# Dummy matmuls around the slots' matmuls: 38 on a constant cleared once, in place of 11 on one cleared there

## The chip, the cores and the metric

The kernel runs on one core of a Trainium2 chip. The metric is the device time of one execution in microseconds (us), lower is better. The engines are TensorE (PE in the rows; PEld is its weight load), VectorE (DVE), ScalarE (ACT), GpSimd (POOL) and SyncE (SP), which here issues most transfers. [...]

## What is computed

Three layers follow each other: attention with a sliding window and a few sink keys, a mixture of eight experts in which each token goes to one expert, and a feed-forward layer of two matrix products.

```python
# attention: batch 2, heads 8, sequence 768, head size 64, window 128, 4 sink keys
scores = where(is_sink | in_window, q @ k.T / sqrt(D), -1e9)
x = (softmax(scores) @ v).transpose(0, 2, 1, 3).reshape(1536, 512)
# experts: 8 of them, 512 -> 1024 -> 512
expert_idx = argmax(normed(x) @ normed(expert_emb).T / tau, axis=1)
for e in range(8):
    m = expert_idx == e
    out[m] = gate_w[m, None] * (maximum(x[m] @ w1[e], 0) @ w2[e])
# feed-forward: 512 -> 2048 -> 512, weights given as float64
h = out @ w_in
y = maximum(0.01 * h, h) @ w_out
```

## The kernel before

The program has three stages. The first, to about 147 us, is attention, with the router's logits, ranks and counts worked in at its end (`router_logits`, `router_rank`, `rank_experts`). It writes the tokens' rows to a buffer in DRAM, `xd`. The second runs the eight experts one after the other, each with a fixed capacity of tokens. The third is the feed-forward layer, in four chunks of 384 tokens.

Between the first and the second stage stands the list of slots: `route` works out which token stands in which slot of which expert, and `id_list` makes the list `ids` by twelve small matmuls (L791) over `c.u` (one-hot rows of the tokens) and `ata` (which block a token falls in, L785). VectorE copies the result to `ids` (L792). Behind that copy VectorE copies the expert's number once more, to `eid2` (L824), and from it SyncE computes the addresses of the first expert's weights from the second quarter on; the first quarter's two loads use `eid` and start earlier. GpSimd uses `ids` to gather the expert's rows from `xd`, 128 at a time, by indirect transfers (L1095).

Weights come in slots of 512 KB (L997), fourteen of which are in use at this point. For most experts each number is cut into a coarse and a fine part: ScalarE casts (L1001), VectorE subtracts (L1002). A product is then three matmuls (`pair`, L1079). The first expert has 128 tokens and runs in `moe_narrow`, in four chunks i. Chunk i's `up` is twelve matmuls into `hp` with slot 2i; ScalarE takes their maximum with zero to `hr` (L1222); `turn` transposes `hr` on TensorE into `th`, and ScalarE (L1230) and VectorE (L1231) cut it into the two parts of `h`; `down` is six matmuls into `acc` with slot 2i+1. `Flow` puts them in the order up 0, turn 0, up 1, down 0, turn 1, up 2, and so on. Ahead of that `turn_rows` transposes the gathered rows on TensorE (`tr`, L1068), and ScalarE and VectorE cut them into `mxT` (L1072, L1073). The rows of the next expert are gathered and turned between the chunks.

The order of the work has two sources. From the second stage on TensorE's instructions run in the order in which the program writes them (`manual_schedule`, L1486). Those of ScalarE, VectorE, GpSimd and SyncE are put in order at build by a planner (`schedule_with_timeline_sim`, L1526): it follows its own timeline and gives an engine, among the instructions that are ready there, the one that the program wrote first. The cuts of the first fourteen slots are written ahead of the first `turn_rows` (`c.work.pop(Q0)`, L1326). On the chip each engine then runs its queue strictly in that order.

`stir` (L1268) is a run of dummy matmuls, 128x128 weights by 512 columns, on a bf16 tile of zeros, whose result nobody reads. Its PSUM tile is one of the four `acc` buffers; their banks were the router's and the attention's until then. There are two places: `WARM[0]` of them ahead of the list's matmuls (L788), `WARM[1]` behind them and ahead of the first `tr` (L1328). The zeros are `c.hot`, cleared by GpSimd as the second stage opens (L1491), in memory of the first stage that has been given back. An attention `stir` of its own (L329) runs seven such matmuls at the very start, on `c.warm`, which VectorE clears at about 1 us (L233) and which lies in a pool of the attention.

Of the kernel before, what the change touches and what calls it, by code (L numbers as in the profile page):

```python
# [9 lines left out]
BF16 = mybir.dt.bfloat16  # L10
# [11 lines left out]
P = 128  # L22
# [116 lines left out]
def attention(c, ctx):  # L139
# [4 lines left out]
    att = ctx.enter_context(tc.tile_pool(name="a_qk", bufs=4))  # L144
# [9 lines left out]
    def load_qk(b, pr, c0=0, n=QB):  # L154
        rk, rq = raws[b, pr] = c.raws[pr % 2]
        for j in range(2):
            nc.sync.dma_start(out=rk[:, c0:c0 + n, j, :],
                              in_=c.k[b, 2 * pr + j].rearrange("(c p) d -> p c d", p=P)[:, c0:c0 + n])
        for j in range(2):
            for twice in range(2):  # L160
                nc.sync.dma_start(out=rq[:, c0:c0 + n, j, twice, :],
                                  in_=c.q[b, 2 * pr + j].rearrange("(c p) d -> p c d", p=P)[:, c0:c0 + n])
# [66 lines left out]
    switches(c, ctx)  # L229
    load_qk(0, 0, 0, 3)  # L230
    load_qk(0, 1, 0, 3)
    c.warm = att.tile([P, 512], BF16, tag="warm", name="warm", bufs=1)
    nc.vector.memset(c.warm, 0.0)  # L233
    setup(c)
    W3 = 2 * P + SINK
# [106 lines left out]
    first, second = group_turns(0, 0)  # L342
    setting = router_setup(c, ctx)
    stir(7)
    n = len(items)
    for _ in range(2):
        first.pop(0)()
    s = 0
    while s < n or after:
# [5 lines left out]
        if s < n:  # L355
            b, g, i, h = items[s]
            k = groups.index((b, g))
            if s in STIR:
                stir(STIR[s])
            j = TURN[b].index(i)  # L360
            at = 4 * j + h
            if s < 3:
                for _ in range(2):
                    if first:
                        first.pop(0)()
            if at in SECOND:
                second.pop(0)()
            if k + 1 < len(groups):
                nb, ng = groups[k + 1]
                if at == 5:  # L370
                    load_qk(nb, 2 * ng, 0, 3)
                    load_qk(nb, 2 * ng + 1, 0, 3)
                    first, then = group_turns(nb, ng)
                if at == 13:
                    load_qk(nb, 2 * ng, 3, 3)
                    load_qk(nb, 2 * ng + 1, 3, 3)
                    load_v(nb, ng)
                if at in FIRST:
                    first.pop(0)()
                if at == 23:  # L380
                    assert not first and not second
                    second = then
            score(b, g, i, h)
# [396 lines left out]
def id_list(c, T, u, q, c0, n, nm):  # L780
# [6 lines left out]
    if nm == "a":  # L787
        stir(c, WARM[0])  # L788
    ip = c.ptr.tile([P, n], F32, tag="tr", name="ip" + nm)
# [152 lines left out]
def slots(c):  # L942

    at = (c.nc.sbuf_usable_end - NSL * 8192) // 32 * 32
    c.slots = [Slot(c, k, at + k * 8192) for k in range(NSL)]
    c.big = c.nc.alloc_sbuf_tensor_at("slot_big", [P, 4096], F32R, offset=at + (NSL - 2) * 8192)[:]
    c.bigf = c.nc.alloc_sbuf_tensor_at("slot_bigf", [P, 4096], F32, offset=at + (NSL - 2) * 8192)[:]
    c.u = c.nc.alloc_sbuf_tensor_at("slot_u", [P, NTT, P], F16, offset=at + (NSL - 2) * 8192)[:]
    end, c.heads = at + (NSL - 2) * 8192, []
    for k in range(8):  # L950
        o = end - (k + 1) * 4 * (KW + 2 * S)
        c.heads.append((c.nc.alloc_sbuf_tensor_at(f"head_k{k}", [P, KW], F32R, offset=o)[:],
                        c.nc.alloc_sbuf_tensor_at(f"head_q{k}", [P, 2, S], F32R, offset=o + 4 * KW)[:]))
    o = end - 8 * 4 * (KW + 2 * S) - 6 * QB * D * 8
    c.raws = [(c.nc.alloc_sbuf_tensor_at(f"raw_k{k}", [P, QB, 2, D], F32, offset=o + 3 * k * QB * D * 8)[:],
               c.nc.alloc_sbuf_tensor_at(f"raw_q{k}", [P, QB, 2, 2, D], F32, offset=o + (3 * k + 1) * QB * D * 8)[:])
              for k in range(2)]
    c.loads, c.work = Loads(c.slots[:NSL - 2]), Work(c.tc)
# [123 lines left out]
def moe_x(c, q0, n, tag, whole=False):  # L1082

    if tag is None:
        xT = c.conv[0].tile([P, 2, 4, n], F32R, tag="dt", name=f"mxT{c.uid()}")
    elif tag == "xb":
        t = 1 if whole else 2
        xT = (c.bigf if whole else c.big)[:, 0:4 * t * n].rearrange("p (t k n) -> p t k n", t=t, k=4)
    else:
        xT = c.mo.tile([P, 1 if whole else 2, 4, n], F32 if whole else F32R, tag=tag, name=f"mxT{c.uid()}", bufs=1)  # L1090
    todo = []
    for k in range(-(-n // P)):
        w = min(P, n - k * P)
        t = c.mo.tile([P, DM], F32, tag="rows" if k < 3 else "y", name=f"rows{c.uid()}", bufs=3)
        c.nc.gpsimd.indirect_dma_start(out=t[0:w], out_offset=None, in_=c.xd[:, :],  # L1095
                                       in_offset=bass.IndirectOffsetOnAxis(ap=c.ids[0:w, q0 + k:q0 + k + 1], axis=0))
        todo.append(lambda t=t, k=k, w=w: turn_rows(c, xT, t, k * P, w, whole))
    return xT, todo
# [163 lines left out]
TAIL = 6  # L1262


WARM = [3, 8]


def stir(c, n):  # L1268

    if n:  # L1270
        t = c.pacc.tile([P, 512], F32, tag="acc", name=f"stir{c.uid()}")
        for _ in range(n):
            c.nc.tensor.matmul(t, lhsT=c.hot[:, 0:P], rhs=c.hot, start=True, stop=True)


def moe(c):
# [44 lines left out]
    def tag(n):  # L1321
        return "xb" if n % 2 else "xa"
# [4 lines left out]
    xT, todo = moe_x(c, BASE[0], WIDTH[0], tag(0), ORDER[0] in WHOLE)  # L1327
    stir(c, WARM[1])  # L1328
    for fn in todo:
# [132 lines left out]
def program(tc, q, k, v, n_sink, window, emb, tau, w1, w2, w_in, w_out, out):  # L1462
    c = Ctx()
    c.tc, c.nc = tc, tc.nc
    c.q, c.k, c.v, c.n_sink, c.window = q, k, v, n_sink, window
    c.emb, c.tau, c.w1, c.w2, c.w_in, c.w_out, c.out = emb, tau, w1, w2, w_in, w_out, out
    c.x, c.xT, c.ids_n = {}, {}, 0

    def uid():
        c.ids_n += 1  # L1470
        return c.ids_n

    c.uid = uid
    with ExitStack() as ctx:
        c.const = ctx.enter_context(tc.tile_pool(name="const", bufs=1))
        c.dram = ctx.enter_context(tc.tile_pool(name="dram", bufs=1, space=DRAM))
        c.xd = c.dram.tile([NT, DM], F32, name="xd")
        with ExitStack() as actx:
            c.masks = actx.enter_context(tc.tile_pool(name="masks", bufs=1))
            c.rt = actx.enter_context(tc.tile_pool(name="r_tile", bufs=2))  # L1480
            slots(c)
            with ExitStack() as bctx:
                if MAN:
                    bctx.enter_context(tc.manual_schedule(engines=MAN))
                attention(c, bctx)
        with tc.manual_schedule(engines={PE}), ExitStack() as mctx:  # L1486
            c.mo = mctx.enter_context(tc.tile_pool(name="m_wk", bufs=1))
            c.conv = [mctx.enter_context(tc.tile_pool(name=f"conv{i}", bufs=1)) for i in range(CONV)]
            c.yT = c.mo.tile([P, 4, YW], F32, name="yT")
            c.hot = c.mo.tile([P, 512], BF16, tag="y", name="hot", bufs=3)  # L1490
            c.nc.gpsimd.memset(c.hot, 0.0)  # L1491
            for kk in range(4):
                c.nc.scalar.activation(out=c.yT[:, kk], in_=c.rowi.to_broadcast([P, YW]), func=AF.Copy, scale=0.0)
            c.pacc = mctx.enter_context(tc.tile_pool(name="ps_acc", bufs=4, space=PSUM))
            c.ph = mctx.enter_context(tc.tile_pool(name="ps_h", bufs=2, space=PSUM))
            c.ptr = mctx.enter_context(tc.tile_pool(name="ps_tr", bufs=2, space=PSUM))
            with ExitStack() as rctx:
                route(c, rctx)
                moe(c)
            c.conv.append(mctx.enter_context(tc.tile_pool(name="convx", bufs=1)))  # L1500
            ffn(c)
        rare = c.nc.values_load(c.rare[0:1, 0:1], min_val=0, max_val=1)
        with tc.If(rare > 0):
            general(c)
# [25 lines left out]
```

## Time and profile before

| what | us |
|---|---|
| three timed runs | 618.84, 621.79, 622.26 |
| their median | 621.79 |
| the profiled execution | 618.77 |
| span of the profiled execution, first to last instruction | 617.0 |
| TensorE busy with matmuls in that span | 588.9 |
| VectorE, ScalarE, GpSimd busy | 396.6, 292.9, 55.1 |

All rows below come from the one profiled execution. Times in them are counted from the first instruction. [...]

### The profile page before, as it was taken

What the parts mean: (1) busy time and instruction counts of PE and PEld (TensorE: products, weight loads), DVE (VectorE), ACT (ScalarE), POOL (GpSimd) and SP (SyncE); (2) the same over time, 40 slices, a digit from 0 to 9 for tenths busy, and PEclk for the clock granted to TensorE, in tenths of its full rate; (3) what the DMA queues carried; (4) which work ended last, traced back from release to release, by engine and by line L of the source; (5) the groups of instructions that cost most, each with busy time, mean ns of one, the idle gap of its engine ahead of it and who ended that gap; (6) DMA issues with size and microseconds to landing.
All of it is one profiled execution on the core that took longest, in us unless ns stands there. A gap on an engine that the chain in (4) does not pass through costs nothing.

```text
span 617.0 us, 10038 instructions
## 1 busy us (share of the span) xinstructions
PE 588.9 (95%) x3603; PEld 537.8 (87%) x3604; DVE 396.6 (64%) x953; ACT 292.9 (47%) x556; POOL 55.1 (9%) x156
## 2 busy tenths in 40 slices
PE   7899999997699999999999999799999999999996
PEld 4799999895599998889989998698998998899894
DVE  7889788856699659997973799953224322242230
ACT  4777787755687444524652463442223322332230
POOL 3011013003122010001000000010000100020001
PEclk7899999996699999999999999999999999999999
DMA  5777560013998683379499600000000100010001
GB/s 119 172 162 173 144 167 2 2 68 110 346 359 302 196 315 106 119 248 372 157 343 338 240 0 2 0 35 18 1 1 0 52 2 0 1 52 0 1 1 56
DMA packets 87994, 73.71 MB, mean 119 GB/s; under 512 B 54024, under 2 KB 70408, under 8 KB 87936
## 3 DMA queue, kind: packets, MB, share of 16 engines
q1 hardware_dynamic: 85824, 66.22, 34.4%
q0 software_dynamic: 2112, 6.75, 3.1%
q8 instruction: 31, 0.51, 0.4%
q14 instruction: 27, 0.22, 0.1%
HBM read 66.67 MB, written 6.29 MB: 118 GB/s over the span
## 4 chain that ended last, share of the span: by engine, by line
PE 87%; DVE 6%; DMA 2%; issue 2%; ACT 1%; SPq 1%; POOL 0%; POOLq 0%; DVEq 0%
PE acc L1079 30%; PE hp L1079 30%; PE xp L298 6%; PE sc L261 4%; PE hp L1176 3%; PE acc L1188 3%; PE tp L280 3%; DMA slot_raw<-in_moe_w 2%; PE tq L196 1%; PE lg L716 1%; PE xp L301 1%; PE tr L1068 1%; PE xTp L697 1%; PE tk L196 1%; DVE slot L1054 1%
## 5 line engine op out<-in xcount | busy, mean ns | idle before, releaser
L1079 PE MATMUL acc<-slot,h 128*128 128x512 f32 x603 | 151.8, 395 | 4.5 <-DVE slot L1054 3.4
L1079 PE MATMUL hp<-fxT,slot 128*128 128x384 f32 x768 | 142.3, 337 | 0.0
L1079 PEld LDWEIGHTS hp<-fxT,slot 128*128 128x128 f32 x768 | 134.9, 188 | 4.7
L1079 PEld LDWEIGHTS acc<-slot,h 128*128 128x128 f32 x603 | 111.8, 188 | 26.5 <-DVE slot L1054 4.1
L1424 DVE TENSOR_TENSOR lk<-hp,lk 128x384 f32<-128x384 f32 x64 | 35.5, 555 | 101.2 <-ACT lk L1423 101.2
L1423 ACT ACTIVATE lk<-hp 128x384 f32<-128x384 f32 x64 | 31.4, 491 | 126.2 <-PE hp L1079 119.3
L1002 DVE TENSOR_TENSOR slot<-slot_raw,slot 128x1024 fp32r<-128x1024 f32 x48 | 58.3, 1222 | 11.4 <-ACT slot L1001 11.1
L1001 ACT CAST slot<-slot_raw 128x1024 fp32r<-128x1024 f32 x48 | 50.0, 1047 | 18.1 <-DMA slot_raw<-in_moe_w 17.8
L268 ACT ACTIVATE p<-p,los 128x288 f32<-128x288 f32 (+2 forms) x96 | 45.6, 504 | 16.8 <-DVE los L266 16.2
L1079 PE MATMUL acc<-h,slot 128*128 128x256 f32 (+2 forms) x288 | 49.0, 319 | 0.0
L1426 DVE TENSOR_TENSOR h<-lk,h 128x384 fp32r<-128x384 f32 x59 | 32.7, 555 | 24.4 <-ACT h L1425 24.4
L261 PE MATMUL sc<-head_k,head_q 128*128 128x288 f32 (+1 forms) x192 | 43.9, 338 | 3.5 <-DVE head_k L207 1.1
L1079 PEld LDWEIGHTS acc<-h,slot 128*128 128x128 f32 x288 | 43.1, 188 | 2.9
L1425 ACT CAST h<-lk 128x384 fp32r<-128x384 f32 x59 | 30.2, 512 | 31.8 <-DVE lk L1424 31.8
L298 PE MATMUL xp<-v,pt 128*128 128x65 f32 x352 | 43.8, 269 | 0.0
L298 PEld LDWEIGHTS xp<-v,pt 128*128 128x128 f32 x352 | 42.6, 192 | 0.1
L1458 POOL DMA_INDIRECT out_y<-y,sid x12 | 12.4, 1037 | 318.6 <-DVE y L1457 298.4
L261 PEld LDWEIGHTS sc<-head_k,head_q 128*128 128x128 f32 x192 | 29.9, 201 | 6.9 <-ACT head_q L216 3.1
L1079 PE MATMUL hp<-slot_big,slot 128*128 128x256 f32 (+1 forms) x192 | 35.4, 333 | 0.0
L1079 PEld LDWEIGHTS hp<-slot_big,slot 128*128 128x128 f32 x192 | 29.8, 189 | 2.7
L280 PE MATMUL tp<-ident,p 128*128 128x128 f32 x176 | 30.2, 278 | 0.0
L1095 POOL DMA_INDIRECT rows<-xd,ids x16 | 18.6, 1162 | 114.0 <-PE tr L1068 110.7
(252 smaller groups left out, 842.6 us busy)
## 6 DMA issues: line engine op xcount, KB each, us to landing
slot_raw<-in_moe_w SPq DMA_DIRECT2D x56, 512.0 KB
slot_wide<-in_moe_w_in SPq DMA_DIRECT2D x8, 1024.0 KB
slot_wide<-in_moe_w_out SPq DMA_DIRECT2D x8, 1024.0 KB
raw_q<-in_q SPq DMA_DIRECT2D x64, 96.0 KB
slot_first<-in_moe_w SPq DMA_DIRECT2D x8, 512.0 KB
raw_k<-in_k SPq DMA_DIRECT2D x32, 96.0 KB
xd<-x SPq DMA_DIRECT2D x12, 256.0 KB
v<-in_v SPq DMA_DIRECT2D x12, 192.0 KB
```

What stands on the lines that cost most here:

```text
L261: nc.tensor.matmul(sc[:, 0:w], lhsT=qt[:, half, i * P:(i + 1) * P], rhs=kt[:, off:off + w], start=half == 0, stop=half == 1)
L268: later(1, lambda: nc.scalar.activation(out=p, in_=p, func=AF.Exp, scale=-1.0, bias=lo))
L280: nc.tensor.transpose(u.t[:, h % 2, n, :], u.p[:, h, o:o + P], c.ident)
L298: nc.tensor.matmul(xp[:, h, :], lhsT=u.pt[h // 2][:, h % 2, n, :], rhs=vT[b, g][:, kb, h, :], start=h == 0 and n == 0, stop=h == 3 and i < ...
L1001: nc.scalar.copy(out=sl.g[0], in_=sl.raw)
L1002: nc.vector.tensor_tensor(out=sl.g[1], in0=sl.raw, in1=sl.g[0].bitcast(F32), op=ALU.subtract)
L1079: c.nc.tensor.matmul(out, lhsT=a[x], rhs=b[y], start=first and n == 0, stop=last and n == 2)
L1095: c.nc.gpsimd.indirect_dma_start(out=t[0:w], out_offset=None, in_=c.xd[:, :], in_offset=bass.IndirectOffsetOnAxis(ap=c.ids[0:w, q0 + k:q0 ...
L1423: nc.scalar.activation(out=raw, in_=hp, func=AF.Copy, scale=0.01)
L1424: nc.vector.tensor_tensor(out=raw, in0=hp, in1=raw, op=ALU.max)
L1425: x = nc.scalar.copy(out=h[:, 0, :], in_=raw)
L1426: y = nc.vector.tensor_tensor(out=h[:, 1, :], in0=raw, in1=h[:, 0, :].bitcast(F32), op=ALU.subtract)
```

## The change

The constant on which the stirs of the second stage run is no longer `c.hot` but `c.warm`. `c.warm` moves from the attention's pool to the pool of constants, so that it lives to the end; `c.hot` and GpSimd's clear of it go. The stirs ahead of the list's matmuls become 10 where they were 3, and those behind them 28 where they were 8.

```diff
@@ -229,7 +229,7 @@
     load_qk(0, 1, 0, 3)
-    c.warm = att.tile([P, 512], BF16, tag="warm", name="warm", bufs=1)
+    c.warm = c.const.tile([P, 512], BF16, name="warm")
     nc.vector.memset(c.warm, 0.0)
@@ -1262,7 +1262,7 @@
-WARM = [3, 8]
+WARM = [10, 28]
@@ -1270,7 +1270,7 @@
         for _ in range(n):
-            c.nc.tensor.matmul(t, lhsT=c.hot[:, 0:P], rhs=c.hot, start=True, stop=True)
+            c.nc.tensor.matmul(t, lhsT=c.warm[:, 0:P], rhs=c.warm, start=True, stop=True)
@@ -1487,8 +1487,6 @@
             c.yT = c.mo.tile([P, 4, YW], F32, name="yT")
-            c.hot = c.mo.tile([P, 512], BF16, tag="y", name="hot", bufs=3)
-            c.nc.gpsimd.memset(c.hot, 0.0)
```

## Rows read from the trace of the kernel before

**Rows 1.** The page: its head, part 2's granted clock, part 4's chain by engine.

```profile
span 617.0 us, 10038 instructions
...
PEclk7899999996699999999999999999999999999999
...
PE 87%; DVE 6%; DMA 2%; issue 2%; ACT 1%; SPq 1%; POOL 0%; POOLq 0%; DVEq 0%
```

**Rows 2.** Chain that ended last, 147 to 164 us: start, duration, what.

```profile
148.85 0.70 POOL hot L1491
...
149.60 0.61 PE stir L1273
...
153.94 9.58 DMA slot_raw<-in_moe_w
```

**Rows 3.** Timeline, 146 to 155: start, duration, engine, line, operation [idle before <-releaser].

```profile
146.50 0.17 PE L733 MATMUL rk<-cum,ones 128*128 128x16 bf16 x1
...
146.80 0.16 DVE L736 TENSOR_TENSOR sel<-rk,oh 128x16 f32<-128x16 f32 x1
...
150.25 0.36 DVE L785 TENSOR_TENSOR ata<-qsel,q 128x192 f16<-128x192 f32 x1
...
150.85 0.51 PE L791 MATMUL ipa<-ata,slot_u 128*128 128x16 f16 x12
...
151.22 3.50 PE L1273 MATMUL stir<-hot 128*128 128x512 bf16 x8
...
151.56 0.15 DVE L824 COPY eid<-eid 1x8 int32<-1x8 int32 x1
...
151.95 1.19 POOL L1095 DMA_INDIRECT rows<-xd,ids  x1 [2.40 <-DVE has L832]
```

**Rows 4.** Windows: busy of PE, PEld, DVE, ACT, POOL, granted clock, DMA share, GB/s.

```profile
154.50:155.00 0.50, 0.22 (x1) 0.00 (x0) 0.00 (x0) 0.50 (x2) 0.29 (x1) 0.99 1.39 399
...
157.50:158.00 0.50, 0.00 (x0) 0.00 (x0) 0.50 (x1) 0.00 (x0) 0.00 (x0) 0.93 0.89 324
...
168.00:168.50 0.50, 0.50 (x3) 0.45 (x3) 0.37 (x1) 0.39 (x3) 0.00 (x0) 0.83 1.06 358
...
158.00:168.20 10.20, 7.62 (x31) 6.70 (x32) 6.15 (x8) 6.17 (x8) 0.95 (x1) 0.50 1.04 366
```

**Rows 5.** Timeline, 158 to 168, columns as in rows 3.

```profile
158.74 1.11 PE L1068 MATMUL tr<-ident,rows 128*128 128x128 f32 x4 [4.02 <-DMA rows<-xd,ids]
159.89 0.59 ACT L1072 CAST mxT<-tr 128x512 fp32r<-128x512 f32 x1 [3.18 <-PE tr L1068]
...
160.53 3.23 PE L1079 MATMUL hp<-slot,mxT 128*128 128x256 f32 x12 [0.68 <-ACT mxT L1072]
...
163.55 1.04 ACT L1001 CAST slot<-slot_raw 128x1024 fp32r<-128x1024 f32 x1 [1.18 <-DMA slot_raw<-in_moe_w]
164.50 0.38 ACT L1222 ACTIVATE hr<-hp 128x256 f32<-128x256 f32 x1
...
167.05 1.05 ACT L1001 CAST slot<-slot_raw 128x1024 fp32r<-128x1024 f32 x1 [0.81 <-DMA slot_raw<-in_moe_w]
167.15 0.42 DVE L1231 TENSOR_TENSOR h<-th,h 128x256 fp32r<-128x256 f32 x1
```

**Rows 6.** Chain that ended last, 165 to 172 us, columns as in rows 2.

```profile
165.62 2.56 PE hp L1079 x12
168.18 1.45 PE acc L1079 x6
...
170.28 1.41 PE hp L1079 x12
```

**Rows 7.** Waits, 170 to 617 us: who <- for whom: total us, times, longest.

```profile
PE acc L1079 <- DVE slot L1054: 3.4, 2, 1.8
```

**Rows 8.** Windows early in the attention, columns as in rows 4.

```profile
19.00:20.00 1.00, 0.03 (x1) 0.06 (x1) 0.90 (x4) 0.66 (x2) 0.00 (x0) 1.00 0.66 149
...
21.00:22.00 1.00, 0.75 (x3) 0.40 (x3) 0.97 (x5) 0.65 (x2) 0.00 (x0) 0.70 0.84 191
```

## Prediction

> **What bounds the kernel now.** I read the page first: TensorE is busy nearly all of the span of 617.0 us, 87% of the chain that ended last lies on it, and the row of the granted clock has a dip besides the one at the start, in its tenth and eleventh slices (139 to 170 us) [rows 1]. [...]
>
> Then the chain of waits through that stretch [rows 2]. The reader is to see two things. TensorE's first stir stands in the chain, and what it waited for is GpSimd's clearing of `hot`, which ended at 149.55. And behind the list comes neither TensorE nor a stir but a transfer of weights, 9.58 us, to 163.5.
>
> Then the timeline of the two places. At the first [rows 3], TensorE has its last router matmul at 146.50, idles, runs three stirs, and begins the list's matmuls at 150.85. Their operand `ata` was there at 150.25 + 0.36 = 150.61, so the three stirs already hold the list up by 0.24. Everything behind hangs on the list: `eid2` (the copy at 151.56), from which the loads of slot 2 onward are addressed, and the row gather at 151.95. At the second [rows 5], the first expert's rows are turned at 158.74. Between 151.22 + 3.50 = 154.7 and 158.7 TensorE does nothing.
>
> [...] From 158.0 to 168.2 it is busy 7.62 us at half speed. That gives the ceiling of any gain there: 7.62 / 2 = 3.8 us, 0.6%.
>
> **The change, part by part.**
>
> *The constant.* GpSimd's clear of `hot` (0.70 us, [rows 2]) goes; `warm` was cleared long before. GpSimd's next job, the gather, waits for the list anyway [rows 3]: worth nothing by itself. But the first stir is freed from 149.55. What is late next is its PSUM buffer: it reuses one that the router's last readers held, and these end at 146.80 + 0.16 = 146.96 [rows 3]; at the earliest it follows TensorE's own last matmul, 146.50 + 0.17 = 146.67. I take 146.95.
>
> *Seven more stirs ahead of the list.* [...] I take +0.3. This is on the path: the list, `eid2`, the loads and the gather all move by it.
>
> *Twenty more stirs behind the list.* They start about 151.6. Before, the clock rose 4.9 us after the first stir (149.6 to 154.5, [rows 2, 4]); with stirs from 146.95 the same lag gives about 152, and the true instant can lie some us to either side. [...] The rows would be there at 158.74 + 0.3 = 159.0. [...]
>
> *What the higher clock is worth.* The rows are turned and the first twelve `hp` matmuls run at full speed: 3.23 us [rows 5] become about 1.7. But nothing waits for that. The next step is ScalarE's `hr`, and ScalarE's queue has the cut of slot 4 ahead of it, whose weights land at 163.53 (it idled 1.18 us for them) and which ends at 164.59 [rows 5]. `hr` comes then, however early `hp` ends. So TensorE waits from about 162 to 165 where it waited from 163.8 to 164.9, on top of a wait of its own for ScalarE's copy of the turned rows, which starts at 159.89 [rows 5]. Does the clock last through that? Early in the kernel it was granted in full while TensorE had nearly nothing to do (0.03 us busy from 19 to 20), and it fell between 21 and 22 [rows 8]; at 158.0 it fell after the idle time behind the stirs [rows 4]. So I expect it to be down again by 165, and the stretch from 165 to 168.2 to run at half speed as before, only later. The value I take for the clock is 0.
>
> [...]
>
> *What is queued differently.* TensorE's order here is as written, but those of ScalarE, VectorE and GpSimd are fixed at build by a planner, with its own idea of when TensorE will be done. It will think the first rows 20 stirs later, so it may put one or more cuts of slots ahead of the copy of the rows or of `hr`. The trace can't show it. Bounds: 0 where the order stays, and for each cut that passes `hr`, from 1.05 (the cut itself, [rows 5]) to (167.05 - 163.55) / 2 = 1.75 us, the pace of the cuts of slots 4 and 6, which both waited for their weights [rows 5]. One cut more would give some 1.4. A gain is not excluded either, as the planner would come nearer to the real times. I take +0.5, a third of one cut.
>
> *Behind it.* From 168 on the chain is TensorE's matmuls, 1.41 to 1.45 us a group at full clock [rows 6], and TensorE waits for VectorE's decoding only 3.4 us in two places [rows 7]. That decoding is queued behind VectorE's own `h` steps, so it moves with TensorE. A shift at 165 therefore arrives at the end one for one.
>
> *Sum.* +0.3 (list) + 0 (stirs behind it) + 0 (clock) + 0.5 (order) = +0.8. The profiled execution took 618.77, 617.0 of it the span; it would take 619.6. It is 3.0 below the median of the three runs. The sum goes on the median: 621.79 + 0.8 = 622.6.
>
> **Rivals.**
>
> *More cuts pass ahead of `hr` (slower).* If the planner lets two pass, `hr` comes after the cut that starts at 167.05 and ends at 168.10 [rows 5], not at 164.50: +3.6, with the delay +3.9: 625.7. It decides from the second cut on. For it: the order already holds `hr` behind one landing. Against it: the planner has its rows wait for the gather too, so that part of the stirs is hidden from it as well.
>
> *The clock holds to 165 (faster).* Then `hp` of the second chunk, 2.56, takes 1.41 [rows 6], but VectorE's `h` (167.15 to 167.57, behind its own cut [rows 5]) holds the third `acc` matmul: 167.57 + 0.3 + 4 x 0.24 = 168.8 for the end of `acc`, against 168.18 + 1.45 = 169.63. A gain of 0.8: 621.0. If the median run also has its 3.0 us over the profiled one from slow matmuls here, and the stirs heal that, 618. For it: the stirs make the engine busy from 147 on without a break. Against it: the waits above.
>
> *The stirs don't raise the clock in time.* [...] Against it: the same zeros raised the clock at 154.5.
>
> **How the numbers follow.** Forecast (delay, clock lost, at most one cut): 0.60, from 621.5 to 624.0. Two cuts or more: 0.17. Clock held: 0.19. Stirs too slow: 0.04. About 0.5%, 3.1 us, is what a measurement of this kernel can tell from no change. Faster by more needs the clock held and most of the median's 3.0 besides: 0.08. Slower by more needs two cuts (0.14 of its 0.17) or slow stirs (0.03): 0.17. Same: 0.75. The range leaves out a tenth on each side: 619.3 to 625.5.
>
> **What would show it.** Right: the list's matmuls near 151.2; the stirs' end near 158; `tr` at about 159.0 with a granted clock of 1.0; `hr` still released behind a cut that waited for its DMA; the clock back at 0.5 before 166. Wrong: 1.0 from 153 to 176; or ScalarE's order with other cuts ahead of the first `mxT` or `hr`; or a list that starts before 150.85.

## The result: slower by 0.6%

| | before | after |
|---|---|---|
| median of 11 runs, us | 621.85 | 624.36 |
| lowest and highest | 618.84, 623.13 | 623.48, 628.07 |
| ratio, 95% interval | | 1.0064 [1.0044, 1.0085] |
| profiled execution, its span | 618.77, 617.0 | 623.48, 621.7 |

The two medians differ by 2.5 us, the profiled executions by 4.7, and the ratio stands for 4.0 (0.0064 x 621.85). That is more than the 0.5% that the prediction took as the least that can be told from no change. The time is inside the forecast range, but the likeliest case was "no change", and the rival on the slow side happened. For the experiments below, medians are of all executions; ratios, against the kernel before in the same session (its medians were 620.0 to 622.1 there), leave out the few executions that took 736 us and more.

The page of the changed kernel answers [rows 1]:

```profile
span 621.7 us, 10091 instructions
...
PEclk7899999997699999999999999999999999999998
...
PE 83%; DVE 8%; DMA 3%; issue 2%; ACT 2%; SPq 0%; POOL 0%; POOLq 0%; DVEq 0%; ACTq 0%
```

The row is the share of its full clock that TensorE was granted; the traces of before and after show it at 0.50 and at 1.00. The dip is not gone: it is in the same two slices, the tenth at 0.7 where it was 0.6. The chain has lost 4 points of TensorE and has 2 more of VectorE and 1 more each of transfers and ScalarE. So TensorE waits more, not less.

The timeline answers [rows 3] and [rows 5]. These are the stirs, the list, the gather and the turning of the rows:

```profile
146.83 4.21 PE L1273 MATMUL stir<-warm 128*128 128x512 bf16 x10 [0.35 <-DVE sel L736]
...
150.88 0.45 PE L791 MATMUL ipa<-ata,slot_u 128*128 128x16 f16 x12
...
151.18 6.20 PE L1273 MATMUL stir<-warm 128*128 128x512 bf16 x28
...
152.61 1.20 POOL L1095 DMA_INDIRECT rows<-xd,ids  x1 [5.50 <-DMA slot_raw<-in_moe_w]
...
159.00 0.63 PE L1068 MATMUL tr<-ident,rows 128*128 128x128 f32 x4 [1.62 <-issue]
```

Up to here all went as meant. The list's matmuls begin at 150.88 (150.85 before), but their operand `ata` was there 0.18 us earlier than before, at 150.43: the ten stirs hold the list by 0.45, where three held it by 0.24. The 28 stirs end at 157.4, and the rows are turned at 159.00 with the clock at 0.99 (157 to 161), in 0.63 us where it took 1.11 at 0.50. Then ScalarE, which cuts the slots and also takes `hr`:

```profile
160.33 1.05 ACT L1001 CAST slot<-slot_raw 128x1024 fp32r<-128x1024 f32 x1 [2.73 <-DMA slot_raw<-in_moe_w]
161.28 0.58 ACT L1072 CAST mxT<-tr 128x512 fp32r<-128x512 f32 x1
163.60 1.05 ACT L1001 CAST slot<-slot_raw 128x1024 fp32r<-128x1024 f32 x1 [1.74 <-DMA slot_raw<-in_moe_w]
164.82 1.05 ACT L1001 CAST slot<-slot_raw 128x1024 fp32r<-128x1024 f32 x1 [0.18 <-DMA slot_raw<-in_moe_w]
166.95 1.04 ACT L1001 CAST slot<-slot_raw 128x1024 fp32r<-128x1024 f32 x1 [1.08 <-DMA slot_raw<-in_moe_w]
167.90 0.38 ACT L1222 ACTIVATE hr<-hp 128x256 f32<-128x256 f32 x1
```

The reader is to see the last line and the one above it. Before, `hr` stood behind the cut of slot 4 and came at 164.50 [rows 5]. Now it stands behind the cut of slot 6. That cut starts when its weights land, at 166.95, and before it started at 167.05 [rows 5]: the transfer is not later, `hr` is only queued behind it. ScalarE idled 1.08 us ahead of that cut, and for the last 0.76 of it the operand of `hr` was done: `hp` ends at 166.19 in the trace. The chain of waits says the same; this part answers [rows 2]:

```profile
155.55 11.38 DMA slot_raw<-in_moe_w
166.95 1.04 ACT slot L1001
168.00 0.29 ACT hr L1222
```

And what became of the clock, by windows (busy time of PE, PEld, DVE, ACT, POOL, then granted clock, DMA share, GB/s), beside [rows 4]:

```profile
151.00:157.00 6.00, 6.00 (x40) 2.82 (x38) 2.79 (x10) 5.97 (x6) 3.10 (x3) 1.00 0.94 297
157.00:161.00 4.00, 1.01 (x6) 0.42 (x4) 2.10 (x2) 1.27 (x2) 0.94 (x1) 0.99 1.02 348
161.00:171.00 10.00, 5.97 (x25) 5.38 (x26) 6.61 (x7) 5.60 (x8) 0.00 (x0) 0.50 1.05 363
```

With the stirs the clock is 1.00 from 151 to 157 and 0.99 from 157 to 161. TensorE is busy only 1.01 us of these last four, and the clock is at 0.50 for the ten that follow. It is back about 171 (0.91 from 171 to 172), where it was back at 168 before (0.83 from 168.0 to 168.5 [rows 4]). That is one fall in one trace; not every wait of TensorE is followed by one, as the early order below shows.

Starts in the two profiled executions, in us:

| | before | after | difference |
|---|---|---|---|
| list (L791) | 150.85 | 150.88 | +0.03 |
| `tr` | 158.74 | 159.00 | +0.26 |
| `hr` of chunk 0 | 164.50 | 167.90 | +3.40 |
| second expert's first `h` | 178.23 | 181.58 | +3.35 |
| its fifth `h` | 189.15 | 193.08 | +3.93 |
| feed-forward, first `lk` | 342.02 | 346.78 | +4.76 |
| end of the span | 617.0 | 621.7 | +4.7 |

3.4 of the 4.7 us arise at one instruction. The rest comes between 182 and 347. That last part is not worked out further: from the second expert's seventeenth `h` to the first `lk`, the profiled executions of one order differ by up to 1.7 (113.1 to 114.8 in the last four kernels below; 112.6 before, 113.3 after).

### The profile page after: what moved, and what is told of

Read it like the earlier page. It is cut to its first block, busy times and chain, and to the rows that moved or that the text cites. A ratio compares the mean times of both kernels' runs of the same rounds, so it can differ in the third digit from the quotient of the medians.

```text
span 621.7 us, 10091 instructions
## 1 busy us (share of the span) xinstructions
PE 594.5 (96%) x3631; PEld 540.1 (87%) x3631; DVE 397.0 (64%) x953; ACT 292.5 (47%) x556; POOL 54.6 (9%) x155
## 4 chain that ended last, share of the span: by engine, by line
PE 83%; DVE 8%; DMA 3%; issue 2%; ACT 2%; SPq 0%; POOL 0%; POOLq 0%; DVEq 0%; ACTq 0%
PE acc L1079 29%; PE hp L1079 29%; PE xp L298 6%; PE sc L261 4%; PE tp L280 3%; DMA slot_raw<-in_moe_w 3%; PE hp L1176 2%; PE acc L1188 2%; PE lg L716 2%; PE tq L196 1%; PE xp L301 1%; DVE slot L1002 1%; PE xTp L697 1%; PE tr L1068 1%; PE tk L196 1%
```

## The experiments

The theory was: the loss is the order of ScalarE's and VectorE's queues, which the planner changed, and not the stirs. The rivals: the stirs delay the list; the clock is worse; the moved constant delays the gather. ScalarE's order in the first expert, with cN the cut of slot N, X the copy of turned rows, r `hr`, h and y as named, and H the wide `h` of the second expert:

```
before    c0 c1 X c2 c3 c4 r c5 h c6 r c7 h X c8 r c9 h X c10 r c11 h c12 H c13 y c14 H
after     c0 c1 c2 c3 X c4 c5 c6 r h c7 r c8 h X c9 r c10 h c11 X c12 r c13 h H c14 c15 y
early     c0 c1 X c2 r c3 h c4 r c5 h X c6 r c7 h X c8 r c9 h c10 H c11 c12 c13 y c14 H
early, y  c0 c1 X c2 r c3 h c4 r c5 h X c6 r c7 h X c8 r c9 h c10 H c11 y c12 H c13
```

To give a kernel one of these orders, each cut and each step of the first expert is told to be issued after the one ahead of it, and after each step a given number of cuts is written. The core of that edit, here for the order of before:

```diff
+START, PACE = 2, dict(X=[3, 1, 1], hr=[1, 1, 1, 1], h=[1, 0, 0, 1], H=[1])
...
+def held(c):
+    ctx = ExitStack()
+    for x in K.last.values() if K.on else []:
+        ctx.enter_context(c.tc.issue_after(x.ins))
+    return ctx
...
-        nc.scalar.activation(out=hr, in_=hp, func=AF.Relu)
+        with held(c):
+            a = nc.scalar.activation(out=hr, in_=hp, func=AF.Relu)
+        pace(c, "hr", a)
```

It adds no computation. No run held the kernel before in its own order, so what the edit itself is worth is not known apart. The kernels without stirs leave out dummy matmuls and no part of the computation.

**After, in the order of before.** The edit above on the changed kernel.

> The changed kernel (10 and 28 stirs on the constant that is cleared once), with ScalarE's and VectorE's queues for the first expert held in the order of the kernel before: two cuts of slots ahead of the copy of the first rows, five ahead of the first hr. Theory A, the order of the cuts costs the time: the loss goes, 621 to 622.5 us against 621.85 before. Theory B, the stirs or the moved constant cost it by themselves: about 624.4, as the changed kernel.

Measured: 621.79 us, 1.0024 [1.0007, 1.0042]. `hr` is at 164.70 and the second expert's first `h` at 178.32 (178.23 before): the 3.4 us are gone. What was left came later: the order was held only to the first H, and behind it the planner put `y` behind the cut of slot 14. The chain there:

```profile
171.20 9.10 DMA slot_raw<-in_moe_w
...
180.33 1.05 ACT slot L1026
181.37 0.49 ACT y L1283
```

**The same, and `y` ahead of the cut of slot 14.** The order of before to its last place shown.

```diff
+            with held(c):
+                a = nc.scalar.copy(out=y, in_=acc[0])
```

> As e1 (changed kernel, queues of the first expert held in the order of the kernel before), and in addition ScalarE's copy y of the first expert's result is held ahead of the cut of slot 14, as it is in the kernel before; in e1 it stood behind that cut, which began at 180.33 when its weights had landed, and the lead from 178 to 189 us grew by 1.5. Theory A (order costs the time, wherever it stands): ratio to before 0.999 to 1.001, first narrow-to-wide shift gone. Theory B (38 stirs cost the rest of e1's loss): 1.0024 as e1.

Measured: 619.18 us, 0.9984 [0.9967, 1.0002]. The constant and the 38 stirs are all there, and no loss is. Its chain is that of [rows 2] again:

```profile
154.50 9.09 DMA slot_raw<-in_moe_w
163.62 1.04 ACT slot L1023
164.67 0.29 ACT hr L1252
```

**Before, in the order of after.** The stirs and the constant of before, PACE set to the order of after.

```diff
+START, PACE = 4, dict(X=[3, 1, 1], hr=[0, 1, 1, 1], h=[1, 0, 1, 0], H=[0])
```

> The kernel before (3 and 8 stirs on the constant that GpSimd clears), with ScalarE's and VectorE's queues for the first expert held in the order of the changed kernel: four cuts ahead of the copy of the first rows, seven ahead of the first hr. Theory A (order): slower by 2.5 to 4.5 us, 624.3 to 626.3, with hr behind the cut of slot 6 near 168. Theory B (stirs or constant): 621.9.

Measured: 625.46 us, 1.0080 [1.0054, 1.0106]. ScalarE's timeline there:

```profile
167.50 1.04 ACT L1026 CAST slot<-slot_raw 128x1024 fp32r<-128x1024 f32 x1 [0.79 <-DMA slot_raw<-in_moe_w]
168.46 0.38 ACT L1253 ACTIVATE hr<-hp 128x256 f32<-128x256 f32 x1
```

With none of the change but the order, the whole loss is there. The order is that of after to the last `h` of the first expert; behind it one cut more stands ahead of H (`c14 H c15 c16 y`), so the ratio can hold a little more than the order of after costs. With the run above this settles the main question: the order is the cause, from both sides.

**The constant alone.** 3 and 8 stirs as before, on `warm` in the pool of constants; the planner free.

```diff
-            c.nc.tensor.matmul(t, lhsT=c.hot[:, 0:P], rhs=c.hot, start=True, stop=True)
+            c.nc.tensor.matmul(t, lhsT=c.warm[:, 0:P], rhs=c.warm, start=True, stop=True)
...
-            c.hot = c.mo.tile([P, 512], BF16, tag="y", name="hot", bufs=3)
-            c.nc.gpsimd.memset(c.hot, 0.0)
```

> Only the constant is changed: 3 and 8 stirs as before, on the constant that is cleared once; GpSimd's clear is gone. The planner chooses the order, and it puts three cuts ahead of the copy of the first rows and seven ahead of the first hr. Theory A (order): slower like the changed kernel, 624 to 626. Theory B in the form that the number of stirs costs the time: 621.9 or a little less, as the list waits for no clear.

Measured: 624.85 us, 1.0068 [1.0043, 1.0093]. ScalarE's timeline there:

```profile
167.19 1.04 ACT L1001 CAST slot<-slot_raw 128x1024 fp32r<-128x1024 f32 x1 [1.12 <-DMA slot_raw<-in_moe_w]
168.14 0.38 ACT L1222 ACTIVATE hr<-hp 128x256 f32<-128x256 f32 x1
```

Seven cuts stand ahead of the first `hr`, as in after, but three and not four of them ahead of X, and the order behind is its own (c0 c1 c2 X c3 c4 c5 c6 r h c7 c8 r). So the 27 added stirs are not needed for the loss. Two further kernels were built and not run, for their order alone: with 10 and 28 stirs on `hot` one cut more stands ahead of the first `hr` (c0 to c3, X, c4, c5, r); with 3 and 8 on `warm`, and GpSimd's clear kept, two more, as in this run. So both halves of the change move the order, and of the constant it is not the clear that is gone. That it is the moment from which the stirs may run is likely, but was not tested by itself, and why the planner decides so was not found out.

**No stirs, in the order of before.**

```diff
-WARM = [10, 28]
+WARM = [0, 0]
```

> The changed kernel with no stirs at all in the two places, and the first expert's ScalarE and VectorE queues held in the order of the kernel before. If the stirs of the kernel before bring nothing (the clock is lost again before the first expert's second chunk): 621.5, the list some 0.2 us earlier. If a warm clock through the list and the first chunk was worth something: above 622.5.

Measured: 619.64 us, 0.9983 [0.9965, 1.0002], the same as with 38 stirs in that order (0.9984). From 157 to 161 the clock was 0.50 here and 1.00 there. With a cut that waits for its weights ahead of `hr`, the higher clock was worth nothing that these intervals can tell.

**Early order: 38 stirs, none, and the stirs of before.** Two cuts fewer stand ahead of each step, so that none which waits for a transfer stands ahead of the first `hr`.

```diff
-START, PACE = 2, dict(X=[3, 1, 1], hr=[1, 1, 1, 1], h=[1, 0, 0, 1], H=[1])
+START, PACE = 2, dict(X=[1, 1, 1], hr=[1, 1, 1, 1], h=[1, 0, 0, 1], H=[3])
```

> The changed kernel (10 and 28 stirs), with fewer cuts ahead of each step than in the kernel before: three ahead of the first hr where there were five, and two fewer at every later step of the first expert; y ahead of the cut of slot 14. Theory A: hr then comes as hp ends, near 162.5, and the warm clock of the first hp counts: 1.5 to 2.5 us faster than before, ratio 0.996 to 0.998. Rival: the landing of the weights holds the later steps, and the gain is given back by the second expert: 0.999 to 1.001.

> As e6 but with no stirs in either place. If a warm clock in the first chunk is worth something once no cut stands ahead of hr, this is 1 to 2 us slower than e6. If the stirs are worth nothing even then, it equals e6, and e4 (no stirs, order of before, ratio 0.998) within 0.1%.

> The kernel before (3 and 8 stirs on GpSimd's constant) with the same early order as e6. If the number of stirs counts under this order: between e6 and e7. If only the order counts: equal to both. In either case hr near 164 or earlier.

Measured: 620.56 us, 0.9999 [0.9979, 1.0019]; 621.36, 1.0019 [1.0003, 1.0036]; 620.92, 1.0010 [0.9988, 1.0031]. Windows of the kernel with 38 stirs:

```profile
157.00:161.00 4.00, 2.74 (x15) 1.24 (x13) 2.04 (x2) 0.59 (x1) 0.60 (x1) 1.00 0.95 310
161.00:171.00 10.00, 8.41 (x56) 7.03 (x55) 7.29 (x9) 7.76 (x13) 1.89 (x2) 1.00 1.05 366
```

and of the one without:

```profile
157.00:161.00 4.00, 1.52 (x6) 1.15 (x6) 1.36 (x2) 1.08 (x2) 0.84 (x1) 0.50 0.99 342
161.00:171.00 10.00, 9.53 (x54) 8.53 (x54) 6.82 (x9) 6.76 (x12) 1.21 (x2) 0.76 1.05 364
```

Now the clock holds, 1.00 throughout, with TensorE busy only 2.74 us of the first four. Counted from the copy of `ids`, because the attention ended at other times in these executions, the second expert's first `h` comes after 24.07 us with 38 stirs, 25.78 without, 25.28 with those of before (26.76 in the kernel before). So behind the list the 38 stirs, with the clock at 1.00, are 1.7 us ahead of none at that point. About 0.55 of it is given back ahead of the list, whose copy comes 1.20 us after `ata` with the ten stirs and 0.65 without. The gain that was expected for 38 stirs did not come: the times are the same within their intervals, as the rival had it, and the chain of the kernel with 38 stirs shows where a lead goes: `y` stands behind the cut of slot 13, whose weights land only at 179.4.

```profile
167.18 12.21 DMA slot_raw<-in_moe_w
...
179.42 1.04 ACT slot L1023
180.47 0.49 ACT y L1283
```

**Early order and early `y`: 38 stirs, none, and 7 in place of 10 ahead of the list.** Of the cuts behind the first H, `y` stands behind that of slot 11 alone.

```diff
-START, PACE = 2, dict(X=[1, 1, 1], hr=[1, 1, 1, 1], h=[1, 0, 0, 1], H=[3])
+START, PACE = 2, dict(X=[1, 1, 1], hr=[1, 1, 1, 1], h=[1, 0, 0, 1], H=[1])
...
-                K.on, K.extra = False, 4
+                K.on, K.extra = False, 6
```

> The changed kernel (10 and 28 stirs) with the early order of the first expert's queues, and y put ahead of the cuts of slots 12 and 13, behind that of slot 11 alone. If the lead of about 2.7 us at H0 was lost only because y stood behind a cut that waited for its weights: the lead is kept through y, and the time is 0.996 to 0.998 of before, 619.4 to 620.6 us at a before of 621.9. Rival, the transfers of the later slots set the pace and the lead goes at whichever cut meets a late transfer: y is early, but by the middle of the second expert the lead is gone and the ratio is 1.000.

> The same order, with no stirs at all (what is left out is dummy matmuls only, nothing of the computation). If the warm clock is worth what stands between the early order with and without stirs (2.1 us at hr of the second chunk, 1.7 us at the first wide h): about 1.5 us slower than the kernel with 10 and 28 stirs, ratio near 0.999 to 1.000. If the transfers set the pace: the same as the kernel with stirs within 0.2%.

> The same order with 7 stirs ahead of the list where there were 10. If the 10 stirs do not hold the list (it began at 150.88 with them, 150.85 before), the time is the same as with 10 within 0.1%. If they hold it by the 0.2 to 0.4 us that other runs showed (151.1 to 151.4), this one is up to 0.4 us faster.

Measured: 619.56 us, 0.9977 [0.9963, 0.9991]; 619.74, 0.9983 [0.9966, 1.0000]; 620.23, 0.9985 [0.9969, 1.0000]. The first is faster than before beyond its interval. Its chain, from the turned rows on VectorE to chunk 0's `hr`:

```profile
153.84 6.13 DMA slot_raw<-in_moe_w
...
159.97 0.70 DVE mxT L1097
...
160.72 2.45 PE hp L1104 x10
...
163.19 0.39 ACT hr L1252
```

No cut that waits for its weights stands ahead of `hr` any more. The profile still puts a transfer ahead of `mxT`, but ScalarE's half of the turned rows, from which that step subtracts, was done only at 159.93, so the transfer holds it by 0.04 at most. The clock did not last here, with the same 38 stirs and the same order up to the second expert's first `h`:

```profile
161.00:165.00 4.00, 3.53 (x20) 3.23 (x20) 1.60 (x2) 1.81 (x4) 0.00 (x0) 0.60 1.05 361
```

The kernel without stirs was expected to be about 1.5 us slower than this one, if the higher clock counts; the medians differ by 0.2, well inside the intervals. The two profiled executions cannot be set beside each other: the rows were turned 9.22 us after `ids` in the one without stirs and 7.36 in the other. With 7 stirs the list begins 0.05 us behind `ata`, with ten 0.43, so the expected 0.4 is there; but the time is no better. The planner, free behind the first expert, put the cut of slot 16 ahead of the second expert's third `h`, and from the first to the fifth `h` it took 16.25 us (175.56 to 191.81) where the kernel with 38 took 12.75 (175.98 to 188.73).

**Early order and early `y`, with the stirs and the constant of before.**

```diff
-WARM = [10, 28]
+WARM = [3, 8]
...
-            c.nc.tensor.matmul(t, lhsT=c.warm[:, 0:P], rhs=c.warm, start=True, stop=True)
+            c.nc.tensor.matmul(t, lhsT=c.hot[:, 0:P], rhs=c.hot, start=True, stop=True)
```

> The stirs and the constant of the kernel before (3 and 8, on the cleared tile) with the same early order and the early y; the first expert's queue is as in the run with 10 and 28 stirs, the planner's order behind the cut of slot 15 differs by one place. If the order alone is what that run won: ratio 0.997 to 0.999, the same as with 10 and 28 stirs. If the longer stirs add to it by keeping TensorE's clock high through the first chunks: 1 to 2 us slower than with them, 1.000 to 1.001, with the granted clock at 0.50 from about 158 to 165.

Measured: 618.38 us, 0.9945 [0.9925, 0.9965], from six executions. With the order alone the kernel before is faster than it was, and than the changed one. The expectation that the longer stirs add to it fell.

**One and the same order, other stirs.** 10 and 26, 3 and 8, 10 and 8, all on the constant. ScalarE's order is that of the run just told, also behind the first expert; the edit is the line of WARM.

> 10 and 26 stirs on the constant, in exactly the ScalarE order that the run with the stirs of before and the early y had, also behind the cut of slot 15 (with 28 behind the list the planner put the cut of slot 17 one step earlier). If the order made that run 0.9945 and the stirs are worth nothing: 0.9945 here too, within 0.002. If the longer stirs cost: 0.997 or more. If they gain once the order is right (the clock at 1.00 in the first chunks): 0.992 or less.

> The same order, 3 and 8 stirs as before, but on the constant: the stirs start near 147 and the list is not held by them. If nothing but the order counts: 0.9945, within 0.002. If the earlier list counts (some 0.3 us): 0.9940. If the constant costs by moving waits onto the gather: 0.9955.

> The same order with 10 stirs ahead of the list and 8 behind it, on the constant. The clock is up early, but 8 stirs at full clock end near 153 and TensorE idles until the rows at 159. If the 28 behind the list are what keeps the clock for the first chunk, the clock is 0.50 again by 159 here, and the time is that of 3 and 8; if 10 and 26 turn out slower than 3 and 8, this tells which of the two places costs: slower here means the 10 ahead of the list.

Measured: 619.39 us, 0.9965 [0.9942, 0.9989]; 619.21, 0.9972 [0.9951, 0.9993]; 620.46, 0.9987 [0.9965, 1.0010]. The clock from 161 to 165, in this order:

```profile
161.00:165.00 4.00, 2.62 (x16) 1.89 (x14) 1.92 (x2) 1.97 (x4) 0.94 (x1) 0.82 1.03 352
```

```profile
161.00:165.00 4.00, 3.23 (x12) 2.71 (x12) 1.92 (x2) 1.62 (x3) 0.95 (x1) 0.50 1.01 346
```

```profile
161.00:165.00 4.00, 3.35 (x13) 2.83 (x14) 1.92 (x2) 1.63 (x4) 0.71 (x1) 0.50 1.02 355
```

With 26 stirs behind the list the clock stays up into the first chunk (0.82 from 161 to 165: 1.00 from 161 to 163, 0.64 from 163 to 165), and with 8 it does not (0.50 in both), as expected. In the time nothing of it is seen: the three ratios lie in each other's intervals, and 3 and 8 on the constant (0.9972) stand beside 10 and 26 (0.9965). The slowest is 10 and 8, which holds the list by 0.58 us behind `ata` and has lost the clock when the rows are turned (0.50 from 159 to 161), but this is not resolved either. A gain or loss of up to some 0.2% by the stirs is not excluded by these intervals; it was not resolved. That 3 and 8 on the constant would come within 0.002 of 0.9945 was expected if nothing but the order counts; it came 0.0027 away. With the clear of before (0.9945) the time is the lowest of all, and the gather gives a reason why that may be so, though its interval overlaps that of 3 and 8 on the constant: where GpSimd still clears `hot`, the gather starts 0.47 to 0.48 us after the copy to `ids` (four traces); where it doesn't, 1.17 to 1.20 (thirteen traces). The rows are turned 7.0 to 7.3 us after `ids` in the four, 7.4 to 9.2 in the thirteen.

## Why the prediction failed

*What bounds the kernel.* Right, and the same line decided: `hr` stands behind a cut whose weights have to land. The prediction saw that in before and reasoned from it that the clock is worth nothing there. The run with 38 stirs and the one with none, in the order of before, are at 0.9984 and 0.9983.

*The constant.* Right that the first stir follows the router's readers (146.83; 146.95 was taken). Wrong that the clear's removal is worth nothing on GpSimd: the gather starts at 152.61 where it started at 151.95 [rows 3], with the list no later. In this execution `tr` came 0.26 later; behind the cut of slot 6 that cost nothing.

*The list.* +0.3 was taken, a term that no run shows. What the runs show in its place is +0.21: the list began 0.03 later, but only because attention ended 0.18 earlier in that execution, and counted from `ata`, ten stirs hold it by 0.45 and three held it by 0.24. The clock rose only as the ten ended (0.81 from 150.5 to 151.0), and they took 4.21 us.

*The 28 stirs behind it.* No run of before shows the 0 that the sum has for them. The trace of after agrees with it: their end was put near 158 and was 157.4, hidden in the wait for the rows, which are turned at 159.00.

*The clock.* Right in its course (0.99 at `tr`, 0.50 from 161 to 171, lost before the second chunk), except that the first `hp` matmuls, taken at full speed, began only at 161.91 and had 0.50. Right in its value, 0, as long as a cut that waits for its weights stands ahead of `hr`.

*What is queued differently.* This is the step that failed. It was taken at +0.5, a third of one cut; two cuts more passed ahead of `hr`, which measured +3.4 there and +4.7 at the end of the profiled execution. The price of the second cut was right: the rival put `hr` at 168.10, it came at 167.90. Its chance of 0.17 was held down by the argument that the planner lets its own rows wait for the gather and so hides part of the stirs. That looked at the wrong half of the change: the constant alone, without a stir more, puts two cuts more ahead of `hr` and brings the loss of 1.0068. A term that the trace of before can't show, bounded from 0 to several us, was given a value near its low end without a reason from a row.

*Behind it.* A shift was to arrive one for one. It arrived as +4.7 for 3.4. The planner's order behind the first expert changed as well, and 0.5 more had come by the second expert's fifth `h`; that this order is the cause of the rest was not shown.

*The sum.* 622.6 forecast, 624.36 measured. With the step in question at the rival's price it was 625.7.

## What to carry to other kernels

Where a planner fixes the queues at build, an edit that adds instructions which nobody waits for is still an edit of every order behind it: compare the engines' orders of both builds ahead of any sum of durations. Look at what stands in an engine's queue ahead of the step that the next engine waits for. Here ScalarE idled 1.08 us for a cut's weights, 0.76 of it with the operand of `hr` done; such a cut set the time, and a higher clock of TensorE in front of it (1.00 against 0.50 from 157 to 161) was worth nothing (0.9984 against 0.9983). Here such cuts were moved behind the short steps, and the seven kernels with the early order and the early `y` were 0.1% to 0.5% faster than before, four of them beyond their interval, also with the old stirs. How much of this is the early order is open: the two kernels held in the order of before with `y` ahead of the cut of slot 14 stand 0.2% under before as well (0.9984 and 0.9983).

## What was not expected of the hardware

The granted clock rose behind matmuls on zeros, as it had in the trace of before (0.50 from 149.5 to 154.5, 0.99 from 154.5 to 155.0 [rows 4]). In after ten of them ran from 146.83, with the clock at 0.50 from 146.0 to 150.5, 0.81 to 151.0 and 1.00 from 151 to 157; in the kernel without stirs and with the early `y` it was 0.50 from 151 to 157. What decides how long it stays was not settled. With 38 stirs it was 0.50 from 161 to 171 in the order of after, and 1.00 there in the early order (620.56 us). The order is not all of it: the kernel with the early `y` has the same order up to the second expert's first `h` and the same stirs, and its clock was at 0.60 from 161 to 165. Nor is the wait between the stirs and the rows: the stirs ended at 159.3 and the rows were turned at 160.5 in the first of these two, at 157.3 and 158.7 in the second. From 151 to 157 the clock was 1.00 in the second and 0.77 in the first. No run varied any of this alone.

The clear of `hot` had taken something over from the gather: without it the gather starts 0.7 us later after the same list, in all thirteen traces. The built programs show what. In that of before, six wait instructions, for transfer queues, VectorE, TensorE and ScalarE, stand on GpSimd's queue ahead of the clear, and the gather waits for VectorE alone. In that of after, five such instructions stand right ahead of the gather, and the one that waits for the list is the fourth of them. How they come to 0.7 us was not measured, and the releaser that the trace names there changes from run to run.
